# Two block products of span 0 in two levels of Strassen, with the results of a tail's first product placed in the buffers of the exponentials

## The chip, the cores and the metric

The kernel runs on one core of one Trainium2 chip. A core has a matrix engine (TensorE, PE in the profile), VectorE (DVE), ScalarE (ACT), GpSimd (POOL) and SyncE (SP); each works through its own instructions in the order in which the program gives them, and they meet at semaphores. The metric is device time in microseconds (us) of one execution; lower is better. The median of the three runs of the kernel before is 1350.4 us.

## The reference, cut to what matters

```python
batch, n_heads, seq, head_dim = 8, 12, 448, 64
q_n, k_n = rmsnorm(q, g_q), rmsnorm(k, g_k)
scores = q_n @ k_n.T / sqrt(head_dim)          # per batch and head: 448 x 448
attn = softmax(scores) @ v
x = attn.transpose(0, 2, 1, 3).reshape(3584, 768)
h = x @ w_in                                   # 768 -> 2048
out = square(maximum(h, 0)) @ w_out            # 2048 -> 768, out: 3584 x 768
```

All of it is in float32. Attention runs per batch and head; its result is the input of a feed-forward block with two matrix products, called here the first product (by `w_in`) and the second product (by `w_out`).

## The kernel before, in words

**Spans.** The 8 batches are handled in 4 spans of two batches. For a span the kernel computes attention (12 pairs of heads), then the first product, then the second product. The second product of span 0, 1 and 2 is not run by itself: its matmuls are woven between the steps of the attention of the next span, so that PE has work while the softmax goes through the other engines. What is left of it when that attention ends is run alone, and then comes the next span's first product.

**One level of Strassen (the Winograd form).** Each product of a span is a 2 x 2 block product done with 7 block products, named `A11, A12, S2, S1, S3, A22, S4` in the order in which the second product takes them (`order2`, L648). The right-hand sides are blocks of the activations (`gT`, 16 rows of 2 x 448 columns) and sums of these (`gC`, three sums of 8 rows), which `combine(f, parts)` (L1036 to L1047) makes on DVE: a call for one `f` and one part makes two subtractions, L1043 and L1044, or L1046 and L1047. In spans 1 and 2 `combine` is called in the first product. In span 0 it is called in the second product, once in every four matmuls of its first 64 (L1178, L1179), 16 calls in all.

**A block product the ordinary way** (L1170 to L1201): three row blocks `m`, each a sum over 8 blocks `c` of a matmul with 128 x 128 weights and 448 columns. After the eighth, DVE (L1195) or, for `A11`, ACT (L1192) takes the bank of PSUM out; where a block of the output is finished, `deliver` (L1253) turns it with a DVE transpose (L1257) and SP stores it with four DMAs (L1260). The weights come in blocks through a ring of five buffers (`load_blocks`).

**A block product in two levels** (L1203 to L1246), which the text calls a tail: row blocks 0 and 1 are again split 2 x 2 and done with 7 products of 4 matmuls on 224 columns (`run`, L1158), and row block 2 stays ordinary (8 matmuls on 448 columns, L1219). The sums that it needs are made on DVE (`add_g`, L1145, four calls) and POOL (`add_weights`, L1150 and L1151, then L1211 and L1212); its four weight blocks come by `load_set` (L1138). The parts are put together on DVE and POOL in the rows `into`, `z` and `y`. `FIRST` says for each of spans 0, 1, 2 how many of the 7 block products are ordinary; the others are tails.

**The attention of spans 1 to 3** (`attention(first)`) takes one pair of heads in five steps, `a` to `e` in this text, each ended by a `yield`:

- a: on PE the values of the pair before (L874), and the last two of the four groups of scores of this pair (L792; the first two were issued just ahead of the values); on ACT their exponentials (L794); on DVE a sum of exponentials (L817) and the sums of squares of a later pair (L745), which ACT copies across partitions (L748)
- b: DVE turns the next pair's queries and keys (L768) and scales (L755, L756); POOL takes a power (L757) and multiplies (L759, two calls)
- c: DVE adds the other exponentials (L817, L815) and finishes the pair before (L910, L912; L912 waits for the factors that the pair before sent through DRAM)
- d: `fold`: DVE reduces the sums of exponentials (L824), and ACT copies the result across partitions (L827)
- e: `factors_of`: DVE (L834 to L836); POOL issues two DMAs through DRAM (L1031, L842) that spread the factors

The exponentials of the next pair's scores stand behind L827 on ACT, and the scores of its step a wait for these exponentials, since `ps_s` has two buffers. There are five buffers for exponentials (`places`): four of two rows of 448 columns, `pr0` to `pr3`, and one more.

**The weaving** is done by the loop at the end: after step number u of the attention (0 to 60) the second product has been advanced to `total * (u + 1) // 61` matmuls, and then by three with each step:

```python
total, done, most = FIRST[span] * HC * HF - (20 if FIRST[span] == 7 else 6), 0, 10 * NPAIR + 1
for u, _ in enumerate(attention(nxt)):
    while done < total * min(u + 1, most) // most + 3 * max(u + 1 - most, 0):
        next(rest)
        done += 1
```

`HC` is 3, `HF` is 8 and `NPAIR` is 6, so `total` is 138 for `FIRST` 6 and 114 for `FIRST` 5.

Of the kernel before, what the change touches and what calls it, by code (L numbers as in the profile page):

```python
# [10 lines left out]
F32 = mybir.dt.float32  # L11
# [376 lines left out]
def attention_then_ffn_bounded(  # L388
# [35 lines left out]
    nc = tc.nc  # L424

    B, H, S, D = q.shape
# [217 lines left out]
        return (A11, A12, S2, S1, S3, A22, S4) if span == f == 0 else range(7)  # L644

    N1 = HF * 7
    FIRST = (6,5,5)
    order2 = (A11, A12, S2, S1, S3, A22, S4)  # L648
    plan, begins = [], {}
    for span in range(NSPAN):  # L650
        begins[span, 1] = len(plan)
        plan += [(w1s[f, i].rearrange("p (c m) -> p c m", c=HC), 2 * (f + 1)) for f in range(HF) for i in order_of(span, f)]
        begins[span, 2] = len(plan)
        if span + 1 < NSPAN:
            plan += [(w2s[i, k, :, :, m * P:(m + 1) * P], 2 * NFC) for o, i in enumerate(order2)
                     for m in range(HC) if o < FIRST[span] or m == HC - 1 for k in range(HF // 4)]

    def load_blocks(upto):
# [447 lines left out]
    def second_product(work, span):  # L1106


        rhs_of = {A11: gT[:, 0:HF, 0:S], S2: gC[:, 1], S1: gC[:, 0], S3: gT[:, 0:HF, S:2 * S],
                  A12: gT[:, HF:, 0:S], A22: gC[:, 2], S4: gT[:, HF:, S:2 * S]}  # L1110
        HK, HS, NB = HF // 2, S // 2, HF // 2 * P
        left, right = slice(0, HS), slice(HS, S)
        sub, add = ALU.subtract, ALU.add
        n = begins[span, 2]
        first, end = FIRST[span], len(order2)
        late = []
        turn[0] += 1

        zone = {end - k: gC[:, k - 1].rearrange("p f n -> p (f n)") for k in (1, 2)}
        tiles = {o: [z[:, k * NB:(k + 1) * NB].rearrange("p (c m) -> p c m", c=HK) for k in range(6)]  # L1120
                 for o, z in zone.items()}
        p1s = [work.tile([P, S], F32, tag="p1", name="p1", bufs=HC) for _ in range(HC)]
        ys = [work.tile([P, S], F32, tag="y", name="y", bufs=1)] + [zone[end - k][:, 6 * NB:6 * NB + S] for k in (2, 1)]
        spared = [gT[:, f, S:2 * S] for f in range(HF)]
        squares_of = [gT[:, HF + k, 0:S].rearrange("p (g n) -> p g n", n=32) for k in range(5)]

        def t_of(o, k):
            rows = gT[:, o % 2 * HF + 2 * k:o % 2 * HF + 2 * k + 2, 0:S]
            return rows.rearrange("p r (h n) -> p r h n", h=2)

        def parts_of(o):
            rhs = rhs_of[order2[o]]
            return [[rhs[:, k * HK:(k + 1) * HK, t * HS:(t + 1) * HS] for t in range(2)] for k in range(2)]

        def load_set(o):
            if o < end:
                for k, (m, h) in enumerate(((0, 0), (0, 1), (1, 0), (1, 1))):
                    nc.sync.dma_start(tiles[o][k], w2s[order2[o], h, :, :, m * P:(m + 1) * P])  # L1138

        def add_g(o, k):  # L1140
            if o < end:
                (b11, b12), (b21, b22) = [[b.rearrange("p (r h) n -> p r h n", h=2) for b in row] for row in parts_of(o)]
                t1, t2, t3, t4 = (t_of(o, k) for k in range(4))
                dst, x, y = ((t1, b12, b11), (t2, b22, t1), (t3, b22, b12), (t4, b21, t2))[k]
                nc.vector.tensor_tensor(dst, x, y, sub)  # L1145
# [4 lines left out]
                nc.gpsimd.tensor_tensor(s1, a21, a22, add)  # L1150
                nc.gpsimd.tensor_tensor(a21, a11, a21, sub)  # L1151

        def send(o):
            for k in range(len(late)):
                ct, *where = late.pop(0)
                deliver(work, span, ct, *where, osb=squares_of[k + 2 * (o - end + 1)] if o > first else None)

        def run(ps, lhs, rhs, start=True):  # L1158
            for c in range(HK):
# [2 lines left out]
                if c % 2:  # L1162
                    yield

        for o, i in enumerate(order2):
            base, more, dst = {A11: (None, None, p1s), A12: (p1s, None, None), S2: (p1s, None, p1s),
                               S1: (p1s, None, ys), S3: (ys, p1s, None), A22: (p1s, None, None),
                               S4: (ys, None, None)}[i]
            where = (HC if i in (S3, A22) else 0), 1 if i in (S3, S4) else 0
            if o < first:  # L1170
                for m in range(HC):
                    ps = bank("ps")
                    for c in range(HF):
                        load_blocks(n + 5)
                        nc.tensor.matmul(ps, stream[n][:, c % 4], rhs_of[i][:, c], start=c == 0, stop=c == HF - 1)  # L1175
                        n += c % 4 == 3
                        at = (o * HC + m) * HF + c
                        if span == 0 and at < 8 * HF and at % 4 == 1:  # L1178
                            combine(at // 4 % HF, (at // 4 // HF,))  # L1179
                        if c == 3:  # L1180
                            send(o)
                        if o == first - 1 and c == 5:
                            if m < 2:
                                load_set(first + m)
                            for k in ((0, 1), (2,), (3,))[m]:
                                add_g(first, k)
                            if m == 2:
                                add_weights(first)
                        if c < HF - 1:
                            yield  # L1190
                    if base is None:
                        nc.scalar.copy(dst[m], ps)  # L1192
                    else:
                        to = dst[m] if dst else work.tile([P, S], F32, tag="ct", name="ct", bufs=1)
                        nc.vector.tensor_tensor(to, base[m], ps, add)  # L1195
                        if more:
                            nc.vector.tensor_tensor(more[m], more[m], ps, add)
                        if not dst:
                            late.append((to, m + where[0], where[1]))
# [15 lines left out]
            send(o)  # L1215
            ps = bank("ps")
            for c in range(HF):
                load_blocks(n + 5)
                nc.tensor.matmul(ps, stream[n][:, c % 4], rhs_of[i][:, c], start=c == 0, stop=c == HF - 1)  # L1219
# [388 lines left out]
```

## Time and profile before

| What | Value |
|---|---|
| median of 3 runs | 1350.4 us (1349.66 to 1351.36) |
| profiled execution | 1349.56 us, of which the span of its instructions is 1347.7 us |
| PE busy | 1325.4 us (98%) |
| DVE busy | 843.6 us (63%) |
| POOL busy | 666.4 us (49%) |
| ACT busy | 485.3 us (36%) |
| granted TensorE clock | 0.999 |
| second product of span 0 with the attention of span 1 | 263.3 to 440.3 us |
| the one tail of span 0 | 440.3 to 456.9 us |
| second product of span 1 with attention, then its two tails | 592.0 to 742.6, to 775.8 us |
| second product of span 2 with attention, then its two tails | 911.0 to 1063.0, to 1096.2 us |

The profile gives busy time, and a group of instructions by its line in the kernel, its engine and its operands. A float32 matmul of this kernel stands in the trace as two instructions, and runs of the same kind are merged: "x16" is eight matmuls. In a row of the timeline the first number is the start, the second the time to the end of the last one, and the bracket at the end says how long the engine sat idle before it and what released it. The last matmul of a run seems to last longer than its share, because its end is modelled; the time of a run is read from its start to the next run's start. In the table of stretches, a row has the stretch, its length, and then for each engine its busy time with the number of instructions.

### The profile page before, as it was taken

Reading aid. Unit: us, or ns where it says so; the run is one execution under the profiler, and the core shown is the slowest. Engines: PE = TensorE matmul, PEld = TensorE weight load, DVE = VectorE, ACT = ScalarE, POOL = GpSimd, SP = SyncE. Lnnn points to the kernel's source line nnn. Section 1 sums busy time; section 2 is a strip of 40 time slices with the busy share of each in tenths; the row PEclk is TensorE's granted clock in tenths of the full one; section 3 lists DMA queues with packets and bytes.
Section 4 is the critical chain, followed back from the end, with each engine's and each line's share of the span. In section 5 each row is a group of like instructions: output and inputs, shape, how many; then the busy total and the mean of one; then the engine's idle time right before and its main releaser. Section 6 shows DMA issues by size and latency. Waiting matters only on the chain.

```text
span 1347.7 us, 17639 instructions
## 1 busy us (share of the span) xinstructions
PE 1325.4 (98%) x5906; PEld 694.1 (52%) x5906; DVE 843.6 (63%) x1325; ACT 485.3 (36%) x938; POOL 666.4 (49%) x539
## 2 busy tenths in 40 slices
PE   8999999999999999999999999999999999999997
PEld 3333445444444655444444845444444665556887
DVE  6999788589777333467877523357777823336563
ACT  7886466544533011345553011235554101111000
POOL 5776533466574222647775412447676522322452
PEclk9999999999999999999999999999999999999999
DMA  9777999655666333446766333345664534431333
GB/s 250 217 217 201 316 360 327 185 128 119 136 132 152 88 88 88 102 112 120 153 132 167 74 96 88 91 114 118 124 132 122 133 87 134 134 88 50 115 102 57
DMA packets 413818, 190.19 MB, mean 141 GB/s; under 512 B 282388, under 2 KB 408724, under 8 KB 413716
## 3 DMA queue, kind: packets, MB, share of 16 engines
q1 hardware_dynamic: 406164, 180.21, 51.3%
q0 software_dynamic: 4736, 8.40, 2.3%
q8 instruction: 49, 0.80, 0.3%
q10 hardware_dynamic: 2816, 0.34, 0.2%
q14 instruction: 53, 0.43, 0.1%
HBM read 155.72 MB, written 33.16 MB: 140 GB/s over the span
## 4 chain that ended last, share of the span: by engine, by line
PE 83%; DVE 7%; ACT 3%; DMA 2%; issue 2%; POOL 1%; SPq 0%; DVEq 0%; POOLq 0%; ACTq 0%
PE ps L1175 19%; PE pd L1083 10%; PE pa L1083 10%; PE pc L1083 10%; PE sc L792 6%; PE pav L874 6%; PE pb L1083 5%; PE ps L1352 3%; PE ps L1219 2%; PE pd L1324 2%; PE pa L1324 2%; PE pc L1324 2%; PE pc L1160 1%; PE pd L1160 1%; PE pa L1160 1%
## 5 line engine op out<-in xcount | busy, mean ns | idle before, releaser
L757 POOL TENSOR_TENSOR half<-half,mhalf 128x28 f32<-128x28 f32 x36 | 185.3, 5148 | 83.2 <-DVE half L756 73.7
L1059 POOL TENSOR_TENSOR gT<-gT 128x448 f32<-128x448 f32 x96 | 93.9, 980 | 259.6 <-ACT gT L1055 259.6
L1175 PE MATMUL ps<-gT,sw 128*128 128x448 f32 x432 | 169.3, 545 | 0.0
L1055 ACT ACTIVATE gT<-gT 128x448 f32<-128x448 f32 x96 | 55.4, 577 | 300.5 <-DVE gT L1098 300.5
L1083 PE MATMUL pa<-xT,sw 128*128 128x448 f32 x384 | 155.1, 540 | 1.6 <-DMA sw<-w1s 1.0
L1175 PE MATMUL ps<-gC,sw 128*128 128x448 f32 x336 | 131.4, 545 | 0.0
L1175 PEld LDWEIGHTS ps<-gT,sw 128*128 128x128 f32 x432 | 80.1, 190 | 87.5 <-issue 86.1
L792 PE MATMUL sc<-qkT 64*64 64x448 f32 (+1 forms) x1152 | 110.6, 497 | 0.5 <-ACT pr L794 0.4
L1083 PEld LDWEIGHTS pa<-xT,sw 128*128 128x128 f32 x384 | 72.6, 190 | 73.0 <-issue 71.6
L583 POOL TENSOR_TENSOR gC<-gC 128x384 f32<-128x384 f32 x64 | 76.3, 1210 | 63.1 <-DVE gC L579 61.3
L1175 PEld LDWEIGHTS ps<-gC,sw 128*128 128x128 f32 x336 | 62.4, 190 | 68.1 <-issue 66.3
L1098 DVE TENSOR_TENSOR gT<-z,pd 128x448 f32<-128x448 f32 x32 | 19.8, 620 | 98.9 <-PE pd L1083 82.0
L794 ACT ACTIVATE pr<-sc 128x896 f32<-128x896 f32 x87 | 76.9, 908 | 12.1 <-PE sc L792 12.1
L1083 PE MATMUL pd<-xT,sw 128*128 128x448 f32 x192 | 77.9, 542 | 1.5 <-DVE z L1090 1.3
L842 POOL DMA_DIRECT2D xT<-factors x72 | 38.1, 534 | 82.9 <-DMA factors<-square 58.5
L1083 PE MATMUL pd<-xC,sw 128*128 128x448 f32 x192 | 77.5, 540 | 0.7 <-DVE gT L1098 0.7
L1083 PE MATMUL pb<-xC,sw 128*128 128x448 f32 x192 | 77.5, 540 | 0.2 <-DVE gT L1098 0.2
L1083 PE MATMUL pc<-xC,sw 128*128 128x448 f32 x192 | 77.4, 539 | 0.0
L1083 PE MATMUL pc<-xT,sw 128*128 128x448 f32 x192 | 77.4, 539 | 0.0
L874 PE MATMUL rest<-pr,vt 64*64 64x448 f32 x348 | 72.7, 537 | 0.0
L874 PE MATMUL pav<-pr,vt 64*64 64x448 f32 x348 | 72.7, 537 | 0.0
L827 ACT COPY quarters<-quarters 32x28 f32<-32x28 f32 x108 | 22.9, 212 | 138.0 <-DVE quarters L824 136.3
(276 smaller groups left out, 2438.7 us busy)
## 6 DMA issues: line engine op xcount, KB each, us to landing
sw<-w1s SPq DMA_DIRECT2D x224, 192.0 KB, 2.4
sw<-w2s SPq DMA_DIRECT2D x106, 256.0 KB, 3.4
w1s<-gC SPq DMA_DIRECT2D x8, 1344.0 KB, 7.8
w2s<-gC SPq DMA_DIRECT2D x8, 1344.0 KB, 6.2
qk<-in_q_dram SPq DMA_DIRECT2D x144, 56.0 KB, 2.5
qk<-in_k_dram SPq DMA_DIRECT2D x144, 56.0 KB, 2.5
xT<-factors POOLq DMA_DIRECT2D x72, 112.0 KB, 3.5
out_dram<-osb SPq DMA_DIRECT2D x124, 56.0 KB, 1.9
```

What stands on the lines that cost most here:

```text
L583: nc.gpsimd.tensor_tensor(*[blocks_of(n)[:, place_of(n, i)] for i in (dst, x, y)], op)
L757: nc.gpsimd.tensor_tensor(half, half, mhalf, ALU.pow)
L792: nc.tensor.matmul(sc[part, h, 0:n], qkT[rows, 0, 1, keys], qkT[rows, 0, 0, of], start=True, stop=True)
L794: nc.scalar.activation(pr, sc[:, :, 0:n], AF.Exp)
L874: nc.tensor.matmul(into, vs[i][rows, h, c, :], probs[i, c][rows, h, :], start=(c == 0), stop=(c == NF), skip_group_check=True)
L1055: nc.scalar.activation(g, src, AF.Relu)
L1059: nc.gpsimd.tensor_tensor(g, g, g, ALU.mult)
L1083: nc.tensor.matmul(ps, stream[n + at][:, c], rhs[:, c], start=first and c == 0, stop=c == HC - 1, skip_group_check=not first)
L1160: nc.tensor.matmul(ps, lhs[:, c], rhs(c), start=start and c == 0, stop=c == HK - 1, skip_group_check=not start)
L1175: nc.tensor.matmul(ps, stream[n][:, c % 4], rhs_of[i][:, c], start=c == 0, stop=c == HF - 1)
L1324: nc.tensor.matmul(ps, lhs[:, c], rhs[:, c], start=first and c == 0, stop=c == HK - 1, skip_group_check=not first)
L1352: nc.tensor.matmul(ps, weights_of(o, m, c // HK)[:, c % HK], rhs_of[i][:, c, part], start=c == 0, stop=c == HF - 1)
```

## The change

In span 0 the sixth block product, `A22`, is a tail too, as in spans 1 and 2: `FIRST` becomes `(5,5,5)`. The buffers and the order of some steps of all three spans' tails change with it: the rows `into`, `third`, `z`, `y` and the turned output rows of the first tail lie in `pr0` to `pr3`, those of the second in the second halves of `gT`'s first eight rows; the four weight blocks of the second tail are loaded within the first tail instead of during `S3`; `add_g` of the first tail starts one row block earlier and goes one call at a time; `add_weights` of the second tail comes three products of four matmuls later. The branches for `FIRST` 4 (`apart`) are not taken by any span.

```diff
-    FIRST = (6,5,5)
+    FIRST = (5,5,5)
...
-        zone = {end - k: gC[:, k - 1].rearrange("p f n -> p (f n)") for k in (1, 2)}
...
-        spared = [gT[:, f, S:2 * S] for f in range(HF)]
-        squares_of = [gT[:, HF + k, 0:S].rearrange("p (g n) -> p g n", n=32) for k in range(5)]
+        zone = [gC[:, k].rearrange("p f n -> p (f n)") for k in range(2)]
...
+        b11, b21, b12 = ([gT[:, r + f, at:at + S] for f in range(HF)] for r, at in ((0, 0), (HF, 0), (0, S)))
+        apart = first == 4
+        exps = [pr[:, h] for pr in places[:NJ] for h in range(2)]
+        homes = {first: exps, first + 1: b21 if apart else b12, first + 2: b12}
...
-        def send(o):
-            for k in range(len(late)):
-                ct, *where = late.pop(0)
-                deliver(work, span, ct, *where, osb=squares_of[k + 2 * (o - end + 1)] if o > first else None)
+        def send():
+            for ct, at, osb in late:
+                deliver(work, span, ct, *at, osb=osb and osb.rearrange("p (g n) -> p g n", n=32))
+            late[:] = []
...
-                        if o == first - 1 and c == 5:
-                            if m < 2:
-                                load_set(first + m)
-                            for k in ((0, 1), (2,), (3,))[m]:
-                                add_g(first, k)
-                            if m == 2:
+                            send()
+                        ahead = (o - first + 1) * HC + m + 1
+                        if ahead >= 0 and c == 5:
+                            if ahead == 1:
+                                load_set(first)
+                            add_g(first, ahead)
+                            if ahead == HC:
                                 add_weights(first)
...
-            rows_of = spared[(end - 1 - o) * 4:(end - o) * 4]
-            into, z, y = rows_of[:2], rows_of[2][:, left], rows_of[2][:, right]
+            home = homes[o]
+            into, third, z, y = home[:2], home[2], home[3][:, left], home[3][:, right]
...
-            third = work.tile([P, S], F32, tag="ct", name="ct", bufs=1)
             nc.vector.tensor_tensor(third, base[2], ps, add)
+            load_set(o + 1)
...
-            add_weights(o + 1)
-            deliver(work, span, third, HC - 1 + where[0], where[1],
-                    osb=rows_of[3].rearrange("p (g n) -> p g n", n=32))
+            deliver(work, span, third, HC - 1 + col, t, osb=home[4].rearrange("p (g n) -> p g n", n=32))
...
             nc.vector.tensor_tensor(into[1][:, left], into[1][:, left], pd, add)
+            add_weights(o + 1)
...
-            late += [(into[m], m + where[0], where[1]) for m in (1, 0)]
-        send(end)
+            late += [(into[m], (m + col, t), home[5 + m]) for m in (1, 0)]
+        send()
...
-            rest = second_product(work, span)
             places_for(work, NJ)
...
             sums_for(work)
+            rest = second_product(work, span)
```

More of the change, by code (lines that the diff above doesn't have):

```diff
@@ L646, in attention_then_ffn_bounded, with order2 @@
     N1 = HF * 7
-    FIRST = (6,5,5)
-    order2 = (A11, A12, S2, S1, S3, A22, S4)
+    FIRST = (5,5,5)
+    def order2(span):
+        return (A11, S2, S1, S3, A12, A22, S4) if FIRST[span] == 4 else (A11, A12, S2, S1, S3, A22, S4)
     plan, begins = [], {}
@@ L654, in attention_then_ffn_bounded @@
         if span + 1 < NSPAN:
-            plan += [(w2s[i, k, :, :, m * P:(m + 1) * P], 2 * NFC) for o, i in enumerate(order2)
+            plan += [(w2s[i, k, :, :, m * P:(m + 1) * P], 2 * NFC) for o, i in enumerate(order2(span))
                      for m in range(HC) if o < FIRST[span] or m == HC - 1 for k in range(HF // 4)]
@@ L1110, in second_product @@
                   A12: gT[:, HF:, 0:S], A22: gC[:, 2], S4: gT[:, HF:, S:2 * S]}
+        order, first = order2(span), FIRST[span]
+        end = len(order)
         HK, HS, NB = HF // 2, S // 2, HF // 2 * P
@@ L1114, in second_product @@
         n = begins[span, 2]
-        first, end = FIRST[span], len(order2)
         late = []
         turn[0] += 1
-        zone = {end - k: gC[:, k - 1].rearrange("p f n -> p (f n)") for k in (1, 2)}
[L1120 to L1123, printed above, removed]
-        spared = [gT[:, f, S:2 * S] for f in range(HF)]
-        squares_of = [gT[:, HF + k, 0:S].rearrange("p (g n) -> p g n", n=32) for k in range(5)]
+        zone = [gC[:, k].rearrange("p f n -> p (f n)") for k in range(2)]
+        tiles = {o: [zone[(first + 1 - o) % 2][:, k * NB:(k + 1) * NB].rearrange("p (c m) -> p c m", c=HK)
+                     for k in range(6)] for o in range(first, end)}
+        b11, b21, b12 = ([gT[:, r + f, at:at + S] for f in range(HF)] for r, at in ((0, 0), (HF, 0), (0, S)))
+        apart = first == 4
+        exps = [pr[:, h] for pr in places[:NJ] for h in range(2)]
+        homes = {first: exps, first + 1: b21 if apart else b12, first + 2: b12}
+        p1s, zs = ([work.tile([P, S], F32, tag="p1", name="p1", bufs=HC * (1 + apart)) for _ in range(HC)]
+                   if k == 0 or apart else None for k in range(2))
+        zs = zs or p1s
+        ys = [work.tile([P, S], F32, tag="y", name="y", bufs=1)] + [z[:, 6 * NB:6 * NB + S] for z in zone[::-1]]
+        rows_of = [zone[0][:, k * S:(k + 1) * S] for k in range(2 * HC)]
         def t_of(o, k):
-            rows = gT[:, o % 2 * HF + 2 * k:o % 2 * HF + 2 * k + 2, 0:S]
-            return rows.rearrange("p r (h n) -> p r h n", h=2)
+            r, at = {first: (0 if apart else HF, 0), first + 1: (0, S if apart else 0), first + 2: (0, 0)}[o]
+            return gT[:, r + 2 * k:r + 2 * k + 2, at:at + S].rearrange("p r (h n) -> p r h n", h=2)
         def parts_of(o):
-            rhs = rhs_of[order2[o]]
+            rhs = rhs_of[order[o]]
             return [[rhs[:, k * HK:(k + 1) * HK, t * HS:(t + 1) * HS] for t in range(2)] for k in range(2)]
@@ L1137, in load_set @@
                 for k, (m, h) in enumerate(((0, 0), (0, 1), (1, 0), (1, 1))):
-                    nc.sync.dma_start(tiles[o][k], w2s[order2[o], h, :, :, m * P:(m + 1) * P])
+                    nc.sync.dma_start(tiles[o][k], w2s[order[o], h, :, :, m * P:(m + 1) * P])
         def add_g(o, k):
@@ L1163, in run @@
                     yield
-        for o, i in enumerate(order2):
-            base, more, dst = {A11: (None, None, p1s), A12: (p1s, None, None), S2: (p1s, None, p1s),
-                               S1: (p1s, None, ys), S3: (ys, p1s, None), A22: (p1s, None, None),
+        for o, i in enumerate(order):
+            base, more, dst = {A11: (None, None, p1s), A12: (p1s, None, None), S2: (p1s, None, zs),
+                               S1: (zs, None, ys), S3: (ys, zs, None), A22: (zs, None, None),
                                S4: (ys, None, None)}[i]
-            where = (HC if i in (S3, A22) else 0), 1 if i in (S3, S4) else 0
+            col, t = (HC if i in (S3, A22) else 0), 1 if i in (S3, S4) else 0
             if o < first:
@@ L1180, in second_product @@
                         if c == 3:
-                            send(o)
-                        if o == first - 1 and c == 5:
-                            if m < 2:
-                                load_set(first + m)
-                            for k in ((0, 1), (2,), (3,))[m]:
-                                add_g(first, k)
-                            if m == 2:
+                            send()
[5 more added lines that the diff above has]
+                            if ahead == HC:
                                 add_weights(first)
@@ L1193, in second_product @@
                     else:
-                        to = dst[m] if dst else work.tile([P, S], F32, tag="ct", name="ct", bufs=1)
+                        if dst:
+                            to, osb = dst[m], None
+                        elif apart:
+                            to, osb = rows_of[m], rows_of[HC + m]
+                        else:
+                            to, osb = work.tile([P, S], F32, tag="ct", name="ct", bufs=1), None
                         nc.vector.tensor_tensor(to, base[m], ps, add)
@@ L1198, in second_product @@
                         if not dst:
-                            late.append((to, m + where[0], where[1]))
+                            late.append((to, (m + col, t), osb))
                     yield
@@ L1214, in second_product @@
                 add_g(o + 1, k)
-            send(o)
+            send()
             ps = bank("ps")
@@ L1243, in second_product @@
             nc.vector.tensor_tensor(into[1][:, left], into[1][:, left], pd, add)
+            add_weights(o + 1)
             yield from run(pc, s4, lambda c: b22[:, c], False)
             nc.vector.tensor_tensor(into[0][:, right], into[0][:, right], pc, add)
-            late += [(into[m], m + where[0], where[1]) for m in (1, 0)]
-        send(end)
+            late += [(into[m], (m + col, t), home[5 + m]) for m in (1, 0)]
+        send()
         yield
```

## The prediction

> **What bounds the kernel now.** First the busy times of the page: PE 98%. Then the table of stretches, for the stages that the change touches.
>
> ```profile
> PE   1325.4 (98%) x5906; PEld 694.1 (52%) x5906; DVE 843.6 (63%) x1325; ACT 485.3 (36%) x938; POOL 666.4 (49%) x539
> ```
> ```profile
> 263.30:440.30 177.00, 176.75 (x1056) 81.47 (x1057) 140.95 (x232) 76.90 (x161) 104.95 (x79) 1.00 0.61 132
> 440.30:456.90 16.60, 16.60 (x73) 13.62 (x72) 8.61 (x14) 0.35 (x1) 5.82 (x6) 1.00 0.27 56
> 592.00:737.70 145.70, 145.64 (x951) 66.57 (x950) 112.65 (x184) 70.66 (x150) 100.73 (x72) 1.00 0.64 140
> ```
>
> The columns are the stretch, its length, then PE, weight loads, DVE, ACT and POOL. PE idles 0.25 us in 177 us of span 0's woven stage, nothing in its tail. So a matmul saved there shortens the kernel, as long as nothing else is then late. In span 0 DVE is busy 80% on average. For its first part, with `combine` on DVE, I read the timeline (start, length, engine, line):
>
> ```profile
> 332.68 1.73 PE L792 MATMUL sc<-qkT 64*64 64x448 f32 x16
> 333.09 1.36 DVE L1047 TENSOR_TENSOR gT<-gT 128x448 f32<-128x448 f32 x1
> 334.38 1.10 DVE L824 TRANSPOSE_TENSOR_REDUCE quarters<-acc 128x28 f32<-128x896 f32 x1
> 335.56 0.69 ACT L827 COPY quarters<-quarters 32x28 f32<-32x28 f32 x3 [2.60 <-DVE quarters L824]
> 336.16 1.70 ACT L794 ACTIVATE pr<-sc 128x896 f32<-128x896 f32 x2
> 337.91 0.98 PE L792 MATMUL sc<-qkT 64*64 64x448 f32 x8 [0.19 <-ACT pr L794]
> ```
>
> This is the only wait of PE on scores there, 0.19 us. Scores were issued at 332.68, but their exponentials (336.16) stood behind L827, which waited for DVE's fold; PE's next scores waited for them. I call **lag** the start of L827 less the start of the next pair's first scores. Here it is 335.56 - 332.68 = 2.88; PE waited 0.19, so PE waits for all lag above 2.7. The lags at the ends of pairs 0 to 5 are -1.4, 0.4, -0.4, 2.0, 2.9, 0.7. Span 0's cover is used up at one place already.
>
> **What is removed: matmuls.** A tail in span 1:
>
> ```profile
> 742.59 1.68 PE L1160 MATMUL pa<-gC 128*128 128x224 f32 x8
> 744.11 6.18 PE L1219 MATMUL ps<-gC,sw 128*128 128x448 f32 x16
> 750.12 1.68 PE L1160 MATMUL pb<-gT,gC 128*128 128x224 f32 x8
> ...
> 759.20 1.68 PE L1160 MATMUL pa<-gT,gC 128*128 128x224 f32 x8
> ```
>
> Eight matmuls of 448 columns take 750.12 - 744.11 = 6.01 us, 0.752 each; the whole tail 759.20 - 742.59 = 16.61. The ordinary way `A22` has 24 matmuls, 24 x 0.752 = 18.05. Saved: 1.44 us, all on PE's path.
>
> **What moves: the weaving is thinner.** 114 matmuls instead of 138 stand within the same 61 steps, so a pair of heads gets 9 or 10 instead of 11 or 12. A pair of 11 lasts 13.89 us (276.35 to 290.25), of which 11 x 0.752 = 8.27 are the second product's; attention's own are 5.62. So a pair will last 5.62 + 9 x 0.752 = 12.4 us, or 13.1 with 10. Span 1 runs this way with no PE wait beyond 0.06 us, but has no `combine`. Span 0 has 16 calls in its first 64 matmuls: over 5.7 pairs before, 6.8 after. DVE's attention work per pair is not less, and its time is shorter.
>
> I walk DVE through the pairs. Prices, from the timeline:
> - From a pair's first scores to L755, with DVE waiting for others: 7.9 (276.35 to 284.31; 304.89 to 312.82).
> - From L755 to the next L827, without extras: 5.0 (284.31 to 290.63 is 6.32, less one `combine` of 1.2; 327.03 to 335.56 is 8.53, less 1.1, 0.56 and 1.83).
> - From L827 to L755 when DVE is late: 4.7 (320.81 to 327.03 is 6.22, less a `combine` of 1.0 and an eviction of 0.5).
> - Extras: a `combine` 1.1 to 1.2, but 1.85 in step c when POOL's L759 runs beside it (332.55 to 334.38), 0.5 to 1.3 in step d (ACT's copies hide a part); an eviction (L1195) 0.55, a transpose (L1257) 0.56.
>
> Checked on pair 4 of before (`combine` in e ahead of it, eviction in a, `combine` and transpose in b, `combine` in c): 2.0 + 4.7 + 1.0 + 0.5 = 8.2 to L755; 8.2 + 5.0 + 1.1 + 0.56 + 1.83 - 13.9 = 2.8; 2.9 is measured.
>
> With 114(u+1)//61 the second product's matmuls (counted from 0) fall so: pair 1: 11 to 19, pair 2: 20 to 28, pair 3: 29 to 38, pair 4: 39 to 47, pair 5: 48 to 56, pair 6: 57 to 66. `combine` stands at 1, 5, ... 61; evictions on DVE at 31, 39, 47, 55, 63; transposes at 35, 43, 51. Lags:
> - Pair 1: L755 at 7.9, `combine` in b: 7.9 + 5.0 + 1.2 - 12.4 = 1.7.
> - Pair 2: `combine` in d before it, a and c: L755 at 1.7 + 4.7 + 0.5 to 1.3 + 1.2 = 8.1 to 8.9; lag 8.1 to 8.9 + 6.2 - 12.4 = 1.9 to 2.7.
> - Pair 3: `combine` in a, eviction in b, `combine` in c: L755 about 8.3; 8.3 + 5.0 + 2.4 - 13.1 = 2.6.
> - Pair 4: `combine` in e, eviction in a, `combine` in b, transpose in c: L755 at 2.6 + 4.7 + 1.6 = 8.9; 8.9 + 5.0 + 1.7 - 12.4 = 3.2: PE waits 0.5.
> - Pair 5: `combine` in d, eviction in e, `combine` in a, transpose in b, `combine` in c: L755 at 2.7 + 4.7 + 2.1 to 2.9 = 9.5 to 10.3; lag 9.5 to 10.3 + 7.4 - 12.4 = 4.5 to 5.3: PE waits 1.8 to 2.6.
> - Pair 6: one `combine` in a, one in c, 13.1 us: below 2.7. From there nothing.
>
> In all 2.3 to 3.1, and up to 0.5 in pairs 2 and 3; I take 3.0. The 0.25 of before goes into it. Bounds: from 0 (span 1 with the same weaving) to 7 (second rival).
>
> [...] Beside POOL's L759, L1047 took 1.36 us, against a median of 0.62; beside the 5.06 us of POOL's L757 (from 327.53) DVE's L817 took 1.05 and two L815 together 1.27, their usual times. [...] The rows show the cost beside L759 only, and the walk goes by them.
>
> **What costs nothing.** The exponentials' buffers are free when the first tail writes them: their last readers on PE are the values of the last pair (435.4 in span 0), issued ahead of it. Without that, the copy of `pa` (L1210, ACT) would wait, and `pb`'s sum behind it, 6 us later. In the first tail four loads of 256 KB now stand in SP's queue behind the stores of L1260 (done at 752.84 in span 1) and two `sw` loads (753.84): issued about 753.9 to 756.6 (2.73 for the four at 731.67), landed 3.4 later (the page's `sw<-w2s`, as large), the first at 757.3, the last at 760.0. PE wants the first at 759.20. POOL's first three calls of 1.27 are then done at 763.8, and PE wants the third's result at 766.73: 2.9 us of cover, the fourth's later; if the loads came 3 us later, each of three spans would lose about 1. The stores and `w1s` loads queued behind these have the ring's five blocks as cover. `add_g` on DVE (1.05 each) is only moved, to where spans 1 and 2 have cover (DVE busy 77%); in span 0 it falls after the 64 matmuls. The end of span 0 gets the order of spans 1 and 2: 12 stores ahead of the `w1s` loads; after span 1 PE waited 0.97 us for such a load (785.96), after span 2 and span 0 not. I take no change, with 1 us either way.
>
> **The sum.** 1349.56 of the profiled execution (span 1347.7 and 1.86 around it) - 1.44 + 3.0 - 0.25 = 1350.9. The median of the runs is 0.84 above that execution: **1351.7 us**, 0.1% more. A measurement of this kernel can tell about 0.2%, 2.7 us, from no change.
>
> **Rivals.**
> - *The cover holds.* DVE's 7.9 to L755 hides more than I think, as in span 1, and nothing waits: 1350.4 - 1.44 - 0.25 = 1348.7. For it: span 1 (DVE 77%). Against it: lag 2.9 before, with 11 matmuls to a pair. 0.20.
> - *The loop through DRAM decides; slower.* L912 waits for factors that pass L757, L759 and two DMAs: 16.5 us from L755 (591.82) to L912 (608.35). With L755 at 9 after the scores, a late `combine` and the fold: 9 + 16.5 + 0.6 + 1.05 + 1.85 - 2 x 12.4 = 4.2, a wait of 1.5 in each of pairs 2 to 5, 6 in all: 1350.4 - 1.44 + 5.75 = 1354.7. It decides once L755 is later than 7.5 with a `combine` between L912 and L824. For it: span 1 has lags up to 2.5 where L912 waits for the DMA (608.35, 1.45 us). Against it: in span 0 L912 hardly waits for a DMA, 1.0 us in the whole stage, as DVE comes late itself. 0.32.
> - *The wait at the ends of spans goes as well.* 1348.7 - 1.0 = 1347.7, from the moved loads and stores. 0.06; two thirds of it faster by more than 2.7.
>
> **How the numbers follow.** The forecast has 0.42; a wait of 2 to 4.4 us is within it, and about one in seven of it comes out above 2.7. Slower: 0.32 + 0.06 = 0.38. Faster: 0.04, and 0.02 of the first rival. Same: the rest, 0.56. The range goes from just under the first rival (1348.4) to past the second, with 1 us for the ends of spans (1355.7).
>
> **What would show it.** The first tail of span 0 in 16.6 us; 28 matmuls of 224 columns more. In its woven stage (177.0 - 18.05 = 159 without waits) PE idle of some 3 us, nearly all as waits of scores (L792) for exponentials (L794) behind L827, late in pairs 4 and 5, gone when `combine` is done; no such waits in spans 1 and 2. Wrong would be: lags below 2.7 throughout; waits spread over pairs 2 to 5 with L912 waiting for DMAs; a PE wait at the start of second tails, for `gC<-w2s`.

## The result, and the profile after

The changed kernel took **1354.8 us** (median of 7 runs, 1353.66 to 1360.68) against 1349.66 us for the kernel before on the same chip (median of 7, 1348.16 to 1351.36). The ratio is 1.0047, with a 95% interval of 1.0034 to 1.0059: slower. The forecast was 1351.7 us, within what could be told from no change. Its range (1348.4 to 1355.7) holds the measured median; its verdict does not hold.

The profiled execution took 1357.41 us, with a span of 1355.5 us: 2.6 us more than the median, so what is worked out from its trace explains more than the median lost. First the page of the changed kernel: the busy time of the engines, and the group of the scores (its idle time, and what ended it, are at the end).

```profile
PE 1329.6 (98%) x5930; PEld 699.5 (52%) x5930; DVE 847.0 (62%) x1333; ACT 485.0 (36%) x939; POOL 673.7 (50%) x546
...
L796 PE MATMUL sc<-qkT 64*64 64x448 f32 (+1 forms) x1152 | 112.8, 503 | 4.7 <-ACT qkT L798 2.8
```

(The line numbers are those of the changed kernel: L796 scores, L798 their exponentials, L831 the copies after the fold, L828 the fold, L916 the multiplication by the factors, L1050 and L1051 a `combine`, L763 POOL's multiplication, L846 the DMAs that spread the factors, L1170 and L1234 a tail, L779 transposes of the first span. Kernels made from the one before have the numbers of before, such as L792 and L912.)

PE idles 4.7 us ahead of scores, and its busy time is 4.2 us more than before, although it has less to do. The table of stretches of the changed kernel says where both stand (the columns are the stretch, its length, then PE, weight loads, DVE, ACT, POOL, the granted clock, the DMA share and GB/s).

```profile
265.83:433.51 167.68, 163.21 (x1010) 72.62 (x1010) 137.57 (x225) 75.88 (x161) 105.95 (x79) 0.98 0.59 125
433.51:466.72 33.21, 33.21 (x145) 27.26 (x144) 18.24 (x29) 0.69 (x2) 13.05 (x14) 1.00 0.47 101
593.72:719.53 125.81, 125.59 (x799) 57.02 (x798) 95.73 (x160) 65.68 (x139) 86.52 (x60) 1.00 0.61 129
350.58:357.00 6.42, 6.42 (x22) 2.54 (x23) 5.67 (x10) 4.87 (x10) 2.48 (x4) 0.51 0.58 121
```

The two tails of span 0 take 33.21 us with PE busy throughout, 16.6 each. Span 1's woven stage hardly idles (0.22 us in 126). In span 0's, PE idles 4.5 us, and from 350.58 to 357 it works at **half its clock** (0.51). Now the timeline of the changed kernel: the ends of pairs 1 and 5.

```profile
290.46 1.74 PE L796 MATMUL sc<-qkT 64*64 64x448 f32 x16
292.25 0.89 DVE L916 TENSOR_TENSOR xT<-half,xT 128x448 f32<-128x448 f32 x1 [1.67 <-DMA xT<-factors]
294.25 0.69 ACT L831 COPY quarters<-quarters 32x28 f32<-32x28 f32 x3 [5.67 <-DVE quarters L828]
295.80 0.61 PE L796 MATMUL sc<-qkT 64*64 64x224 f32 x8 [0.97 <-ACT pr L798]
...
343.60 1.74 PE L796 MATMUL sc<-qkT 64*64 64x448 f32 x16
345.48 0.63 DVE L916 TENSOR_TENSOR xT<-half,xT 128x448 f32<-128x448 f32 x1 [1.05 <-DMA xT<-factors]
346.56 1.36 DVE L1051 TENSOR_TENSOR gT<-gT 128x448 f32<-128x448 f32 x1
349.04 0.69 ACT L831 COPY quarters<-quarters 32x28 f32<-32x28 f32 x3 [5.93 <-DVE quarters L828]
350.58 2.57 PE L796 MATMUL sc<-qkT 64*64 64x224 f32 x16 [2.61 <-ACT qkT L798]
```

Read it as in the prediction: lag is the start of L831 less the start of the next pair's first scores. Pair 1 has 294.25 - 290.46 = 3.79, and PE waits 0.97 (and 0.19 at the next scores); pair 5 has 349.04 - 343.60 = 5.44, and PE waits 2.61. In both, DVE stood in L916 for factors that a DMA had not yet brought, with the fold behind it (in pair 5 a `combine` too, ahead of the fold).

**The ledger.** I use one length, the *stage*: from the first scores of span 0's weaving to the next first product. It is 193.69 us before (263.23 to 456.92) and 200.89 after (265.83 to 466.72): +7.20. The rest of the profiled difference of 7.85 is +2.60 ahead of the stage, where the two programs do the same (a half clock in the first 30 us, mean 0.94 against 1.00; more below), and -1.95 behind it, of which 1.2 is the first product after span 1: before waited 0.97 there for `sw<-w1s`, after did not.

Inside the stage the beat is read from one pair's first scores to the next pair's. Attention's own 5.62 us and 0.752 for each woven matmul, as in the prediction, make it 12.39 with 9 and 13.14 with 10. What a pair lasts beyond that I call its *excess*. The changed kernel's first seven pairs last 12.24, 12.39, 14.01, 13.64, 12.55, 12.94 and 19.04; the first has 11 matmuls and no values of a pair before it, so the formula doesn't hold for it; before's first pair lasts 13.12 with 13 matmuls, which makes 11.62 with 11. So the excesses are 0.62, 0, 1.62, 0.50, 0.16, 0.55 and 5.90, in all 9.35. Before has one pair with an excess, of 15.36 with 12 matmuls: 0.72. So -1.44 - 0.72 + 9.35 = 7.19, against the 7.20 measured.

### The profile page after: what moved, and what is told of

Its sections match the earlier page's. It is cut to its first block, busy times and chain, and to the rows that moved or that the text cites. A ratio compares the mean times of both kernels' runs of the same rounds, so it can differ in the third digit from the quotient of the medians.

```text
span 1355.5 us, 17719 instructions
## 1 busy us (share of the span) xinstructions
PE 1329.6 (98%) x5930; PEld 699.5 (52%) x5930; DVE 847.0 (62%) x1333; ACT 485.0 (36%) x939; POOL 673.7 (50%) x546
## 4 chain that ended last, share of the span: by engine, by line
PE 82%; DVE 8%; ACT 4%; DMA 2%; issue 2%; POOL 0%; SPq 0%; ACTq 0%; DVEq 0%; POOLq 0%
PE ps L1185 17%; PE pd L1087 11%; PE pa L1087 10%; PE pc L1087 10%; PE sc L796 6%; PE pav L878 5%; PE pb L1087 5%; PE ps L1366 3%; PE ps L1234 3%; PE pd L1338 2%; PE pc L1338 2%; PE pa L1338 2%; ACT gT L808 1%; PE pa L1170 1%; PE pd L1170 1%
## 5 line engine op out<-in xcount | busy, mean ns | idle before, releaser
L761 POOL TENSOR_TENSOR half<-half,mhalf 128x28 f32<-128x28 f32 x36 | 186.6, 5182 | 74.3 <-DVE half L760 68.8
L796 PE MATMUL sc<-qkT 64*64 64x448 f32 (+1 forms) x1152 | 112.8, 503 | 4.7 <-ACT qkT L798 2.8
L1185 PE MATMUL ps<-gC,sw 128*128 128x448 f32 x288 | 114.9, 553 | 0.0
L1185 PEld LDWEIGHTS ps<-gC,sw 128*128 128x128 f32 x288 | 54.0, 193 | 61.3 <-issue 60.5
L798 ACT ACTIVATE pr<-sc 128x896 f32<-128x896 f32 x87 | 76.7, 906 | 11.9 <-PE sc L796 11.9
L846 POOL DMA_DIRECT2D xT<-factors x72 | 38.0, 532 | 84.4 <-DMA factors<-square 56.4
L831 ACT COPY quarters<-quarters 32x28 f32<-32x28 f32 x108 | 22.9, 212 | 144.1 <-DVE quarters L828 142.3
```

What stands on the lines that cost most here:

```text
L761: nc.gpsimd.tensor_tensor(half, half, mhalf, ALU.pow)
L796: nc.tensor.matmul(sc[part, h, 0:n], qkT[rows, 0, 1, keys], qkT[rows, 0, 0, of], start=True, stop=True)
L798: nc.scalar.activation(pr, sc[:, :, 0:n], AF.Exp)
```

## Experiments

Three theories stood at first: DVE is late because the weaving is thinner (the forecast's), the new order and buffers of the tails cost the time, or the loop of the factors through DRAM does. When the half clock was seen, a second question joined them: does it follow from a long wait of PE, or is it chance?

**The order and buffers alone.** The changed kernel with the old count.

```diff
-    FIRST = (5,5,5)
+    FIRST = (6,5,5)
```

> The changed kernel with FIRST (6,5,5): span 0 keeps one tail, all the moved buffers, loads and sums of the change stay. Theory DVE (the thinner weaving makes DVE's fold late in span 0, PE waits for exponentials behind it, and after a long wait PE runs at half clock): no waits beyond those of before, 1349.7 within 1 us. Rival ORDER (the moved loads, sums or buffers cost the time): most of the 5.1 us stays, 1353 or more. Rival LOOP (the loop of the factors through DRAM is too long for a pair of 12.4 us): as DVE, 1349.7.

Measured: 1350.58 us, ratio 1.0007 (0.9998 to 1.0017). The stage is 193.68 us, as before (193.69). Its row of the table of stretches:

```profile
265.01:442.09 177.08, 176.82 (x1058) 81.53 (x1057) 140.88 (x232) 76.89 (x161) 103.88 (x79) 1.00 0.61 132
```

At the old count the order and the buffers cost nothing that shows. As the whole cause this theory falls.

**The tail alone.** The kernel before with the new count.

```diff
-    FIRST = (6,5,5)
+    FIRST = (5,5,5)
```

> The kernel before with FIRST (5,5,5): only span 0's second tail and its thinner weaving, none of the moved buffers, loads and sums. DVE and LOOP: like the changed kernel, 1353.5 to 1357, with a wait of over 2 us at the end of pair 5 of span 0 and a granted clock of 0.5 for some us behind it. ORDER: 1348 to 1349.

Measured: 1353.32 us, ratio 1.0024 (1.0013 to 1.0035); stage 198.45, 4.76 over before. Timeline, and stretches:

```profile
349.03 0.61 PE L792 MATMUL sc<-qkT 64*64 64x224 f32 x8 [2.19 <-ACT qkT L794]
```
```profile
348.00:350.00 2.00, 0.78 (x12) 0.38 (x16) 1.04 (x4) 2.00 (x4) 0.60 (x1) 0.90 0.85 130
350.00:352.00 2.00, 2.00 (x9) 0.60 (x10) 2.00 (x3) 0.53 (x2) 0.00 (x1) 0.50 0.71 123
352.00:354.00 2.00, 2.00 (x5) 0.89 (x5) 2.00 (x4) 1.90 (x6) 1.06 (x2) 0.75 0.48 118
```

The same wait in pair 5, and a half clock behind it. If a mean is a mix of 0.50 and 1.00, the stretch at 0.90 was at 0.50 for a fifth of its length; so counted it is 0.4 + 2.0 + 1.0 = 3.4 us. So the sixth tail brings most of the loss without the new order.

**The thinning alone.** The kernel before with 114 matmuls in the weaving and the other 24 run by themselves behind it; no second tail.

```diff
-            total, done, most = FIRST[span] * HC * HF - (20 if FIRST[span] == 7 else 6), 0, 10 * NPAIR + 1
+            total, done, most = min(FIRST[span], 5) * HC * HF - (20 if FIRST[span] == 7 else 6), 0, 10 * NPAIR + 1
```

> The kernel before with only the weaving of span 0 thinned: total is 114 instead of 138, the other 24 matmuls follow after the attention; no second tail in span 0, nothing else moved. Theory THIN (the thinner weaving alone makes PE wait): span 0's stage from the first scores to the next first product, 193.7 us before, gets 5 to 9 us longer, with the long wait at the end of pair 5; time 1354 to 1358. Rival TAIL (the second tail itself costs): as before, 1349 to 1350.

Measured: 1358.72 us, ratio 1.0064 (1.0050 to 1.0079); stage 200.15, 6.46 over before. The waits of pair 5 (2.41 us) and of pair 2 (0.70) are back, with 3.4 us at half clock behind the first (0.81, 0.50 and 0.84 in the windows of 2 us from 348). No tail is added here: what hurts is that fewer matmuls stand between the steps of attention.

**`combine` spread over more matmuls.** The changed kernel with one call in six matmuls for one half of the partitions, then one in five for the other.

```diff
-                        if span == 0 and at < 8 * HF and at % 4 == 1:
-                            combine(at // 4 % HF, (at // 4 // HF,))
+                        if span == 0 and at < 6 * HF and at % 6 == 1:
+                            combine(at // 6, (0,))
+                        if span == 0 and 6 * HF <= at < 11 * HF and at % 5 == 4:
+                            combine((at - 6 * HF) // 5, (1,))
```

> The changed kernel with combine in span 0 spread thinner: part 0 once in 6 matmuls (to 43) and part 1 once in 5 (49 to 84), instead of once in 4; the same 16 calls, the same result. A pair then holds 1.5 to 2 calls instead of 2 to 3. DVE: lags under 2.7 but for one or two pairs, waits of scores in span 0 under 1 us in all, no half clock, 1349.66 - 1.44 = 1348 to 1349, faster than both. LOOP: the waits stay where L916 waits for the DMA, 1352 or more. ORDER: 1353 or more.

Measured: 1350.86 us, ratio 1.0007 (0.9998 to 1.0017); stage 193.32, 0.37 under before. Its weaving, in the table of stretches:

```profile
266.15:426.25 160.10, 159.49 (x1009) 72.04 (x1009) 136.81 (x225) 76.25 (x161) 104.91 (x79) 1.00 0.62 131
```

No wait of scores is above 0.20 and the clock is full: the whole loss is gone, so it is DVE's crowding in the pairs with `combine`. It did not turn into the gain that was expected, though: excesses of 0.63 in the first pair, 0.38 and 0.36 in two others, and 0.40 later eat the 1.44 that the tail saves. (-1.44 - 0.72 + 1.77 = -0.39; -0.37 is measured.)

**No factors from DRAM.** The changed kernel with those DMAs left out for pairs 0 to 6 (its output is then not the reference's).

```diff
-                nc.gpsimd.dma_start(sums["out"][i % 2], sums["square"][0:2 * S // 32, 1])
-                spread(i)
+                if first > 2 * NPAIR or i > first + 6:
+                    nc.gpsimd.dma_start(sums["out"][i % 2], sums["square"][0:2 * S // 32, 1])
+                    spread(i)
```

> The changed kernel without the factors' two DMAs through DRAM for pairs 0 to 6 of span 0's woven attention (those pairs are scaled by what lies in xT). DVE: L916 waits for nothing, the wait of 1.6 us after pair 1 goes, but pair 5 still ends with a lag over 3.5 and a wait of 1 us or more; 1350 to 1353. LOOP: all waits of scores go, 1348 to 1349. ORDER: 1353 or more.

Measured: 1349.54 us, ratio 1.0001 (0.9991 to 1.0010); stage 195.84, 2.15 over before. The lag of pair 1 is 1.89 instead of 3.79, that of pair 5 is 3.72 instead of 5.44, and the clock is full (0.998 over the whole execution, 0.999 before). The wait that is left in pair 5, in the timeline:

```profile
346.24 0.61 PE L796 MATMUL sc<-qkT 64*64 64x224 f32 x8 [0.90 <-ACT qkT L798]
```

So the crowded DVE by itself makes 0.9 us of pair 5's wait, and the late factors the rest. With the DMAs, POOL's and the queues' work for them is gone too. The time is under the 1350 to 1353 expected, and why the kernel is no slower than before at a stage 2.15 longer stays open.

**A late fold, made by hand.** In the kernel before, extra reductions ahead of the fold of pair 4 (their results are overwritten by it). One, then three:

```diff
+                for _ in range(1 if first == NAT and i == first + 4 else 0):
+                    nc.vector.tensor_reduce(sums["quarters"][:, 0],
+                                            sums["acc"].rearrange("p h q -> p (h q)").rearrange("p (n k) -> p n k", k=32),
+                                            AX, ALU.add, apply_transpose=True)
```

> The kernel before, with DVE's reduction L824 done once more (1.0 us, the same result) ahead of the fold of pair 4 of span 0's woven attention, where the lag is 2.9. Theory CLOCK (a wait of PE of some 2 us or more brings the granted clock down to one half for some us behind it, a shorter one doesn't): lag 3.9, a wait of 1.2 us, clock 1.0, stage 193.7 + 1.0 = 194.7. Rival NOCLOCK (the half clock comes by chance, not from the wait): the same, 194.7.

> The same with the reduction done three times more: lag 5.9, a wait of 3.2 us. CLOCK: half clock behind it for 6 us, stage 193.7 + 3.0 + 3.0 = 199.7, in nearly every execution, so that the time is over the one of f_delay1 by some 5 us. NOCLOCK: stage 196.7, 2 us over f_delay1.

One: 1351.59 us, ratio 1.0013 (1.0003 to 1.0023), stage +1.15. Three: 1354.36 us, 1.0031 (1.0020 to 1.0042), stage +5.08. The wait of the scores with one, with one and a half (the next experiment), and with three, each from its own timeline:

```profile
338.66 0.61 PE L792 MATMUL sc<-qkT 64*64 64x224 f32 x8 [1.21 <-ACT pr L794]
```
```profile
340.85 0.61 PE L792 MATMUL sc<-qkT 64*64 64x224 f32 x8 [1.89 <-ACT pr L794]
```
```profile
341.81 0.61 PE L792 MATMUL sc<-qkT 64*64 64x224 f32 x8 [3.50 <-ACT pr L794]
```

The third has a half clock behind it, and not the others (1.00). In the table of stretches of the kernel with three (at half clock for 0.7 + 2.0 + 0.7 = 3.4 us, counted as above):

```profile
342.00:344.00 2.00, 1.81 (x17) 0.57 (x12) 2.00 (x4) 1.20 (x3) 0.60 (x1) 0.83 0.27 43
344.00:346.00 2.00, 2.00 (x3) 0.82 (x3) 2.00 (x3) 1.91 (x6) 1.05 (x2) 0.50 0.08 30
346.00:348.00 2.00, 2.00 (x6) 1.01 (x5) 1.84 (x6) 1.61 (x3) 1.31 (x1) 0.82 0.23 85
```

Expected was a stage of 199.7 us and 5 us between the two kernels; 198.77 and 2.8 came. The direction is right, the size was not.

**Between the two.** One extra reduction of 896 columns and one of 448, one profiled run.

```diff
+                    nc.vector.tensor_reduce(sums["quarters"][:, 0, 0:S // 32],
+                                            sums["acc"].rearrange("p h q -> p (h q)")[:, 0:S].rearrange("p (n k) -> p n k", k=32),
+                                            AX, ALU.add, apply_transpose=True)
```

> The kernel before with one and a half extra reductions ahead of the fold of pair 4 (one of 896 columns, one of 448): the wait of that pair's scores should lie between the 1.21 us of one extra (no half clock behind it) and the 2.19 us of the tail alone (half clock behind it): 1.6 to 1.8. CLOCK: if what counts is how long PE stands, this says on which side of 1.7 us the drop begins; either a stage of 195.4 to 195.6 us at clock 1.00 throughout, or some 1.7 to 3.4 us more with 3.4 to 6.8 us at 0.50.

Measured: a wait of 1.89 and a stage of 195.51, +1.82, at full clock throughout; 1353.37 us in that one run. So in this stage the clock stayed at 1.00 after a wait of 1.89 us and went to 0.50 after one of 2.19 (the first 30 us of the same traces show no such sharp bound; see the last section). The pair with the wait has 17.18 - 14.64 = 2.54 of excess, for 1.89 + 0.19 in the rows; with one extra it had 16.51 - 14.64 = 1.87 for 1.21 + 0.19. In both, the wait cost **0.46 us more than its rows say**.

**Matmuls kept for the gap.** The changed kernel, four matmuls moved ahead of pair 5's wait.

```diff
+            if first == NAT and i == first + 6:
+                yield True
...
-            for u, _ in enumerate(attention(nxt)):
+            u = -1
+            for gap in attention(nxt):
+                for _ in range(4 if gap else 0):
+                    next(rest)
+                    done += 1
+                u += not gap
```

> The changed kernel with four matmuls of the second product put ahead of the wait at the end of pair 5 of span 0 (between that pair's values and the next scores) and left out of the steps after it; nothing else. THIN with CLOCK: PE has 3 us of work there, the wait of 2.6 us and the half clock go, 1354.8 - 2.6 - 3.1 = 1349; the wait of pair 1 stays. NOCLOCK: 1352 (the wait goes, the half clock stays as often as before). If the wait only moves on by one pair: 1353 or more.

Measured: 1354.55 us, ratio 1.0031 (1.0016 to 1.0045); stage 198.38. The big wait and the half clock are gone, but a wait of 1.21 stands one pair later, pair 1's stays, and the tails take 1.2 us longer. The wait moved on rather than vanish.

**`combine` spread, and two matmuls ahead.** The spreading is the edit shown above. To close the first pair's gap of 0.63:

```diff
-                while done < total * min(u + 1, most) // most + 3 * max(u + 1 - most, 0):
+                while done < min(total, total * min(u + 1, most) // most + (2 if span == 0 else 0)) + 3 * max(u + 1 - most, 0):
```

> The change with its combine of the last block products spread as in c_spread (one half of the partitions every six matmuls, the other every five), and with two matmuls ahead from the first pair's first step. THIN with CLOCK: in c_spread the weaving stage took 193.32 us against 193.69 before and its first pair still waited or ran 0.65 us long, with one matmul where before has two between the first and later scores. Here that goes: stage 192.5 to 192.8, no wait of 1 us at the scores, no half clock in the stage, so 1.0 us under the kernel before: 1349 to 1350, ratio 0.999 to 1.000. If the first pair's 0.65 us is not the missing matmul but the order of the tail: stage 193.3 as in c_spread, ratio 1.0005.

Measured: 1355.57 us, ratio 1.0035 (1.0023 to 1.0047): a miss. The first pair does lose its gap (13.13 us with 13 matmuls; before, 13.12). But two other places wait instead, in the timeline:

```profile
346.14 0.61 PE L796 MATMUL sc<-qkT 64*64 64x224 f32 x8 [0.68 <-ACT qkT L798]
...
440.68 1.78 PE L1170 MATMUL pd<-gT,gC 128*128 128x224 f32 x8 [1.07 <-DVE pr L1252]
```

The stage of this trace is 195.47, 1.78 over before. That is not all of the 5 us of the median; the other runs have no trace, and the rest stays open. No version tried beats the kernel before.

**The changed kernel again, twice more.** Unaltered; the third time for one trace.

> The changed kernel once more, unaltered, beside the kernel before. CLOCK: the wait of over 2 us in pair 5 stands in this execution too, and the granted clock of the 3 to 7 us behind it is 0.5; the stage is 197 to 201 us, 3.4 us apart or not by whether the half clock lasts one stretch of 3.4 us or two; ratio 1.003 to 1.006. NOCLOCK: the half clock stood by chance in that one profile; here the pair that waits 2.6 us has clock 1.0 behind it, stage 197.5, and the ratio is 1.003 all the same.

> The changed kernel a third time, for its trace. The factors' arrival varies between executions: pair 5 waited 2.61 us in the first trace (L916 1.05 us late and L1051 at 1.36 us) and 0.87 in the second (neither). If that decides, a pair-5 wait above 2 us comes with a late L916 and a half clock behind it, one below 1.3 us with neither, and the stage is 200 to 201 us in the one case and 196.5 in the other. If the wait is over 2 us without a late factor, the fold alone makes it.

Measured: the second set gave 1356.22 us (1350.81 to 1358.15), ratio 1.0039 (1.0026 to 1.0053). Its profiled execution took 1350.81 us, the third 1358.57. The same program, the same pair 5; second trace, then third, from the timelines:

```profile
341.66 1.73 PE L796 MATMUL sc<-qkT 64*64 64x448 f32 x16
342.54 0.62 DVE L916 TENSOR_TENSOR xT<-half,xT 128x448 f32<-128x448 f32 x1
343.62 0.62 DVE L1051 TENSOR_TENSOR gT<-gT 128x448 f32<-128x448 f32 x1
345.35 0.69 ACT L831 COPY quarters<-quarters 32x28 f32<-32x28 f32 x3 [3.13 <-DVE quarters L828]
346.90 0.61 PE L796 MATMUL sc<-qkT 64*64 64x224 f32 x8 [0.87 <-ACT qkT L798]
```
```profile
342.82 1.73 PE L796 MATMUL sc<-qkT 64*64 64x448 f32 x16
344.63 0.63 DVE L916 TENSOR_TENSOR xT<-half,xT 128x448 f32<-128x448 f32 x1 [0.98 <-DMA xT<-factors]
345.17 1.38 DVE L1050 TENSOR_TENSOR gC<-gT,gC 128x448 f32<-128x448 f32 x1
346.46 1.36 DVE L1051 TENSOR_TENSOR gT<-gT 128x448 f32<-128x448 f32 x1
348.93 0.69 ACT L831 COPY quarters<-quarters 32x28 f32<-32x28 f32 x3 [6.29 <-DVE quarters L828]
350.48 0.61 PE L796 MATMUL sc<-qkT 64*64 64x224 f32 x8 [3.29 <-ACT qkT L798]
```

In the second trace the factors were there: no wait at L916, both halves of the `combine` in 0.62, lag 3.69, PE waits 0.87, and the stage is 196.50 us. In the third L916 is 0.98 late, which puts the `combine` beside POOL's L763 (345.12 to 347.34), so it takes 1.38 + 1.36; lag 6.11, PE waits 3.29, and the stage is 200.98. The third stage is as expected. The second is not: a wait of over 2 us and a stage of 197 to 201 us were expected of it. Nor does it tell CLOCK from NOCLOCK, as it has no long wait in pair 5. The later of the two spreading DMAs was issued equally early in the first trace and the second, 2.9 us ahead of the scores. What differed was the way to landing: at worst 4.7 us in the first, 5.1 in the third, and 3.5 in the second. In the one trace with `combine` spread none of this decides: L916 waits 0.73 us at the end of pair 2 there, and no lag passes 2.6.

## Why the prediction was wrong, point by point

**Removed matmuls, order, buffers: right.** Each tail of span 0 takes 16.6 us with no idle PE, the saving of 1.44 stands, and the order alone gives a ratio of 1.0007. At the ends of the spans the one wait of before (0.97 us, after span 1) is gone in the first trace; it is gone too in the kernel with the tail alone, which has the old order, so the new order is not needed for that.

**The walk of DVE: near in pairs 1 to 4, too long in pair 5, and blind to late factors.** Lags by the walk, and in the three traces of the changed kernel:

| Pair | walk | first | second | third |
|---|---|---|---|---|
| 1 | 1.7 | 3.79 | 3.79 | 3.79 |
| 2 | 1.9 to 2.7 | 2.67 | 2.67 | 2.67 |
| 3 | 2.6 | 2.33 | 2.32 | 2.32 |
| 4 | 3.2 | 2.72 | 2.73 | 2.72 |
| 5 | 4.5 to 5.3 | 5.44 | 3.69 | 6.11 |
| 6 | below 2.7 | -0.83 | 1.82 | -0.02 |

That PE waits for all lag above 2.7 held to 0.2 us everywhere. In pair 5 the walk counts no late factors and has 4.5 to 5.3. Where none were late the lag is 3.69 (second trace) and 3.72 (no factors from DRAM), so the walk is 0.8 to 1.6 us too long; that the first trace has 5.44 is luck, as late factors made up the difference.

What failed first is the sentence "in span 0 L912 hardly waits for a DMA, 1.0 us in the whole stage, as DVE comes late itself". It was read off the beat of before. There DVE comes to pair 1's L912 7.5 us after the later of the two spreading DMAs was issued, and that DMA landed in 4.2. At the thinner beat pair 0's fold comes 2.1 us later against the next scores (lag 0.72, was -1.4), its factors are issued that much later, and DVE comes 5.0 to 5.5 us after the issue. In the three traces of the changed kernel the DMA took 6.3 to 6.8 us, and DVE stands 1.3 to 1.8 us in L916. The beat alone doesn't decide it: in the kernels with the tail alone and the thinning alone, at nearly the same lag (0.74), it landed in 4.9 and 5.0, pair 1 has a lag of 1.89 and no wait, and the late factors come at pair 2 instead (0.57 and 0.69 us). Here are the landings of pair 0's factors in the first trace, then those with the tail alone and its L912:

```profile
DMA to landing us min/median/max: 3.8/5.2/6.7
DMA to landing us min/median/max: 3.0/3.9/4.9
290.37 0.63 DVE L912 TENSOR_TENSOR xT<-half,xT 128x448 f32<-128x448 f32 x1
```

Why these DMAs took longer in the changed kernel no run shows. So the second rival's mechanism was there, though in pairs 1 and 5 rather than 2 to 5; its 1354.7 us comes near the median partly by luck, as its four equal waits did not come.

**The step that failed: the term of +3.0 for PE's waits.** It took a wait at its own length and nothing else. Excess in the first seven pairs of the three traces, taken apart:

| Part of the excess, us | first | second | third |
|---|---|---|---|
| waits in the rows of the scores | 4.35 | 2.80 | 5.22 |
| beyond the rows | 2.17 | 2.17 | 2.17 |
| half clock | 2.83 | 0 | 1.70 |
| in all | 9.35 | 4.97 | 9.09 |

The first line is the term that I sized, and 3.0 lies among its values, partly by luck: without factors from DRAM the rows have 1.67. The second is that each pair in which the scores' turn is broken loses up to half a microsecond which no row names (0.46 in the two experiments that made such a wait by hand), and I had rows alone. I had the means to see it: the one pair of before with waits of 0.25 lasts 15.36 us where the formula has 14.64. The third is what pair 5 has beyond its rows and these 0.46 (5.90 - 2.61 - 0.46; 5.64 - 3.29 - 0.19 - 0.46); it follows waits of 2.61 and 3.29 us, and is 0 after the 0.87 of the second trace. Taken at 5 to 9.4 less the 0.72 of before, the sum would have come out 3 to 7 us over before.

**Cause.** Shown: the thinning alone makes a loss of this size (stage +6.46); spreading `combine` takes it away (-0.37), and leaving out the factors' DMAs takes most of it (+2.15 is left of +7.20). Order and buffers do nothing at the old count. At the new count they go with the factors' being late at pair 1 and not at pair 2, and the excess of pairs 1 to 3 is 2.12 with them against 1.25 and 1.35 without. Shown in three traces: whether the factors land in time decides between a wait of 0.87 and one of 2.6 to 3.3. Open: how often each of the two happens in executions without a trace, and so how the median splits; why pair 0's factors took longer to land; and the median of the version with two matmuls ahead.

**DVE beside POOL: as the walk had it.** In the three traces the subtractions of a `combine` were slowed only beside L763, from 0.62 to between 0.84 and 1.38, as the row of before had shown. Beside L761 they took at most 0.67 in the first trace, two of them 0.62 each in its 5.50 us from 274.27.

## What to carry to other kernels

If matmuls are woven between the steps of another stage, each one removed (0.752 us here) also shortens the time that hides the slower engines: check the fold, and the transfers that start after it, at the new beat and not at the old one. Price a wait of the matrix engine from the length of a whole period with such a wait, not from the idle time in its row (0.46 us too little here), and allow for a half clock if the wait nears 2 us: here 1.95 us was enough once, and in the woven stage a half clock cost 1.5 to 2.8 us. Spreading the slow engine's extra work over more of the stage recovered the loss here, but left no gain, as the saving of 1.44 us is 0.1%.

## What the runs showed of the hardware that was not expected

Waits of PE of about 2 us and more were often followed by a half clock. In the woven stage waits of 0.97, 1.21 and 1.89 us left the granted clock at 1.00; those of 2.19, 2.41, 2.61, 3.29 and 3.50 us were each followed by a stretch at half clock (the lowest window of 2 us has 0.50, and 0.54 behind the 3.29). Counted as with the tail alone, it lasted 3.4 us in four traces and about 6.8 us in the first of the changed kernel (the windows from 350 to 357). It cost 1.5 to 1.7 us in the former and 2.8 in the latter, by the pairs' excess.

Length alone does not decide it. In the first 30 us of all 14 traces PE waits once for 1.9 to 3.0 us ahead of transposes (L779, or L775). Two of these waits, each with the stretch behind it, first from the thinning alone, then from the kernel with one extra reduction:

```profile
21.45 0.96 PE L775 MATMUL pt<-ident,qk 112*128 112x112 f32 x4 [1.95 <-ACT qkT L777]
22.00:24.00 2.00, 2.00 (x9) 0.86 (x9) 2.00 (x3) 0.99 (x2) 0.08 (x1) 0.50 1.09 347
21.55 0.60 PE L775 MATMUL pt<-ident,qk 112*128 112x112 f32 x4 [2.21 <-ACT qkT L777]
22.00:24.00 2.00, 2.00 (x12) 0.83 (x12) 2.00 (x3) 0.98 (x2) 0.00 (x0) 1.00 1.10 349
```

Here 1.95 us was followed by half clock and 2.21 was not; nor was 2.35 in the second trace of the changed kernel. Both places together have 12 waits from 1.89 to 2.35 us, six of them with a half clock behind, and eight of 2.41 us or more, all with one. What decides in the band between is open.

So a half clock in the first 30 us comes and goes between executions of the same code: the mean there is 1.00 in the profiled execution of before and in the second of the changed kernel, 0.94 in the first, and 0.94 also in the kernel with the order alone. The start of span 0's weaving, at 263.23 us in before and 263.89 in the second, is at 265.83 in the first and 265.01 with the order alone; nothing in this belongs to the change.
